# Token mix in three contraction passes over all batches, with mixing matrices transposed in 32x32 blocks on the Vector engine

## The chip, the cores and the metric

The kernel runs on one core of one Trainium2 chip. The metric is the device time of one execution in microseconds (us). Engines are named as the profile names them: PE is the Tensor engine's matmuls, PEld its weight loads (they overlap PE), DVE the Vector engine, ACT the Scalar engine, POOL GpSimd, SP the Sync engine. A name with q at its end (POOLq, SPq) is the sequencer of that engine.

Two words are used throughout. A *block* is 128 rows of the output tokens; there are 33. A *piece* is one block times 384 columns, which is one accumulator tile.

## The reference

Eight batches of 4224 tokens with 192 channels go through a causal depthwise convolution and then through a "phase" mixer.

```python
# x: (8, 4224, 192); weight: (8 heads, 7 taps), softmax over the taps
x = causal_conv(x, softmax(weight))          # 8 groups of 24 channels, one filter each
theta = x @ w_theta                          # 192 x 192
zr, zi = x * cos(theta), x * sin(theta)
y = einsum('ts,bsd->btd', w_tok_r, zr) \
  + einsum('ts,bsd->btd', w_tok_i, zi)       # two 4224 x 4224 matrices
u = x + y
out = u + maximum(u @ w_ch, 0)
```

The token mix is nearly all of the work. It contracts 4224 tokens, twice, for 8 x 192 = 1536 columns. The matrices lie in DRAM as (t, s) in float32. A PE matmul contracts over partitions, so it needs them as (s, t): somebody has to transpose them.

## The kernel before

The kernel before works on four batches at a time, in two rounds. Each round first builds `za_r` and `za_i` for all 4224 tokens of its four batches, and keeps them in SBUF. Then it runs over the 33 blocks. In the first round it transposes the matrices on PE and stores the transposed copy in DRAM. In the second round it loads that copy.

```python
# first round only: transpose 33 tiles of each matrix for the next block
for m, (stage, wt, evac_on_act) in enumerate(((stg_r, wt_r, False), (stg_i, wt_i, True))):
    for base in range(0, NSC, NTG):                      # NTG = 8
        pT = psT2.tile([P, NTG * P], BF16, name="pT", tag="pT")
        for k in range(nb):
            nc.tensor.transpose(pT[:, k * P : (k + 1) * P],
                                stage[:, cch * P : (cch + 1) * P], ident)      # L298
        if evac_on_act: nc.scalar.activation(out=dst, in_=src, func=AT.Copy)   # L306
        else:           nc.vector.tensor_copy(out=dst, in_=src)                # L308
    eng.dma_start(out=wtcache[m, tcc], in_=wt[:])
# ... (both rounds) the mix of one block: 132 matmuls of 384 columns
for cch in range(NSC):                                   # 33
    for m, (wt, zz) in enumerate(((wt_r, za_r), (wt_i, za_i))):
        nc.tensor.matmul(y0, lhsT=wt[:, cch, :], rhs=zz[:, cch, 0:2, :], ...)  # L344
        nc.tensor.matmul(y1, lhsT=wt[:, cch, :], rhs=zz[:, cch, 2:4, :], ...)  # L351
# ... the tail of one block: y + x, 8 PE transposes, matmuls with w_ch, relu, store
```

The line numbers in the comments are those of the profile. Whole file:

## Time and profile before

| Before | |
|---|---|
| time, median of 2 runs | 2003.06 us (2000.9 to 2005.22) |
| span of the profiled run | 1999.5 us |
| PE busy | 1843.1 us, 92% |
| set-up, convolution and phase of batches 0–3 | about 0 to 222 us |
| mix of batches 0–3, with matrix transposes | about 222 to 1119 us |
| phase of batches 4–7 | about 1119 to 1242 us |
| mix of batches 4–7 | about 1242 us to the end |

The stages can be read off the page. Its first part gives the busy time of each engine. Its second part cuts the span into 40 slices of 50 us, and each digit is the busy share in tenths. PEclk is the clock granted to PE in tenths of full speed.

```profile
PE 1843.1 (92%) x13522; PEld 1210.1 (61%) x13522; DVE 488.1 (24%) x1029; ACT 373.2 (19%) x630; POOL 71.6 (4%) x119
...
PE   2666799999999999999999677999999999999998
...
PEclk9888899999999999999999755999999999999999
```

PE is saturated, except in the first five slices and in the three around 1150 us, where the clock falls to half as well. These are the two phase stages. The view by windows puts numbers to a piece of each stage. Its columns are the busy time of each engine (with instruction counts), the clock, the share of the DMA engines' time that is busy, and GB/s.

```profile
core 0: us, PE busy (x) PEld busy (x) DVE busy (x) ACT busy (x) POOL busy (x), PEclk, DMA share, GB/s
700.00:950.00 250.00, 249.03 (x1956) 161.65 (x1955) 48.02 (x90) 43.06 (x54) 9.56 (x18) 1.00 0.71 184
1160.00:1250.00 90.00, 68.43 (x459) 55.41 (x457) 73.68 (x183) 50.59 (x104) 0.00 (x0) 0.54 0.19 54
1400.00:1700.00 300.00, 300.00 (x1961) 184.23 (x1960) 37.74 (x67) 11.80 (x14) 0.00 (x0) 1.00 0.34 126
```

In both mix stages PE leaves next to nothing idle, at full clock. So a shorter mix stage has to come from fewer or shorter PE instructions. The first round has some to give. These are the costliest groups of the matrix transposes (busy us and mean ns, then the idle time of that engine before them and what ended it):

```profile
L306 ACT ACTIVATE wt_i<-pT 128x1024 bf16<-128x1024 bf16 (+1 forms) x165 | 130.1, 884 | 140.2 <-PE pT L298 140.2
...
L298 PE MATMUL pT<-ident,stg_r 128*128 128x128 bf16 x1089 | 90.3, 224 | 8.9 <-DMA stg_r<-in_moe_w_tok_r_dram 8.4
L308 DVE COPY wt_r<-pT 128x1024 bf16<-128x1024 bf16 (+1 forms) x165 | 94.2, 588 | 16.1 <-PE pT L298 16.1
...
L298 PE MATMUL pT<-ident,stg_i 128*128 128x128 bf16 x1089 | 87.0, 218 | 1.4 <-ACT wt_i L306 0.7
```

How long a block takes is best read as the distance between its eviction and that of the next block. The timeline of DVE shows it. Its columns are start, duration, engine, line, operation; the square brackets hold the idle time before. The first two lines are from the first round, the last two from the second:

```profile
1042.61 0.56 DVE L364 TENSOR_TENSOR u_10258<-y_10124,xrt 128x384 f32<-128x384 f32 x1 [21.50 <-PE y_10124 L344]
...
1069.84 0.56 DVE L364 TENSOR_TENSOR u_10518<-y_10384,xrt 128x384 f32<-128x384 f32 x1 [21.50 <-PE y_10384 L344]
...
1512.75 0.56 DVE L364 TENSOR_TENSOR u_14321<-y_14183,xrt 128x384 f32<-128x384 f32 x1 [15.10 <-PE y_14183 L344]
...
1535.45 0.56 DVE L364 TENSOR_TENSOR u_14491<-y_14353,xrt 128x384 f32<-128x384 f32 x1 [15.10 <-PE y_14353 L344]
```

That is 27.2 us per block against 22.7 us, so the transposes cost 4.5 us per block.

**A ledger of PE's time.** For each matmul in the trace, take the time from its start to the start of the next. The Trainium skill ("TensorE: Matmul & The Clock Gate", Back-to-back issue gap) gives N/2.4 + 2.5 ns for N moving columns at full clock, 162.5 ns for N = 384. It means matmuls without the weight loads of a real stream, but the trace agrees: the 132 mix matmuls of a block take 21.5 us, 163 ns each. The sum of N/2.4 + 2.5 over all PE instructions is called the *arithmetic* below. What is spent beyond it is called the *loss*. Loss is then waiting, or matmuls at a lower clock. In the kernel before, the arithmetic is 1726.3 us (1415.8 mix, 121.6 matrix transposes, the rest convolution, phase and tail). The first matmul starts at 14.3 us. The losses of the four stages are 126.9, 34.3, 83.9 and 7.1 us. Where a stage is cut moves some 3 us between it and its neighbour.

### The profile page before, as it was taken

The numbers are of one execution on the slowest core, as the hardware profiler recorded it, in microseconds if no ns is written. First come the engines' busy times: TensorE is split into PE (matmuls) and PEld (weight loads), VectorE is DVE, ScalarE is ACT, GpSimd is POOL, SyncE is SP. The second block draws the span as 40 slices with busy tenths as digits, with TensorE's granted clock in tenths as the row PEclk, the third lists the DMA queues.
The fourth block names the chain that finished last, engine by engine and source line by source line (L and its number), as shares of the span: only waits on it lengthen the run. The fifth ranks groups of instructions, "written<-read, shape, count | busy, mean of one in ns | idle before, by whom it ended". The sixth has DMA issues, their size and how long they took to land.

```text
span 1999.5 us, 30320 instructions
## 1 busy us (share of the span) xinstructions
PE 1843.1 (92%) x13522; PEld 1210.1 (61%) x13522; DVE 488.1 (24%) x1029; ACT 373.2 (19%) x630; POOL 71.6 (4%) x119
## 2 busy tenths in 40 slices
PE   2666799999999999999999677999999999999998
PEld 1655566666666666666666466666666666666665
DVE  7555222221122221122221397111111111111111
ACT  2677311111111111111111165000000000000000
POOL 2111000000000000000000000000000000000000
PEclk9888899999999999999999755999999999999999
DMA  6999766667766667766664321223333323333331
GB/s 103 154 155 153 187 174 174 172 181 192 197 177 171 170 182 192 196 178 169 172 181 147 131 63 48 111 111 111 142 134 112 111 111 143 134 111 111 113 144 37
DMA packets 122179, 287.66 MB, mean 144 GB/s; under 512 B 41776, under 2 KB 96704, under 8 KB 96704
## 3 DMA queue, kind: packets, MB, share of 16 engines
q0 software_dynamic: 44432, 84.58, 25.5%
q1 hardware_dynamic: 63360, 123.29, 17.6%
q10 hardware_dynamic: 14256, 77.86, 9.6%
q8 instruction: 105, 1.72, 0.3%
q14 instruction: 26, 0.21, 0.0%
HBM read 259.94 MB, written 110.30 MB: 185 GB/s over the span
## 4 chain that ended last, share of the span: by engine, by line
PE 82%; issue 9%; DVE 4%; DMA 2%; POOL 2%; ACT 2%; DVEq 0%; POOLq 0%; SPq 0%; ACTq 0%
PE pT L298 5%; PE v L385 2%; POOL xcur L186 1%; PE v L392 1%; PE th_ps L239 1%; DVE xTa L233 1%; PE tU L376 1%; PE th_ps L246 1%; PE tU L377 1%; DMA stg_r<-in_moe_w_tok_r_dram 1%; PE y_12313 L344 1%; PE y_12314 L351 1%; DVE th_sb L254 1%; PE y_10806 L344 1%; PE y_16564 L351 1%
## 5 line engine op out<-in xcount | busy, mean ns | idle before, releaser
L351 PEld LDWEIGHTS <-wt_i 128*128 128x128 bf16 x2178 | 213.2, 98 | 137.3 <-issue 7.1
L344 PEld LDWEIGHTS <-wt_i 128*128 128x128 bf16 x2178 | 213.3, 98 | 130.5 <-issue 0.5
L351 PEld LDWEIGHTS <-wt_r 128*128 128x128 bf16 x2178 | 213.3, 98 | 129.4 <-issue 1.4
L344 PEld LDWEIGHTS <-wt_r 128*128 128x128 bf16 x2178 | 213.3, 98 | 128.6 <-issue 0.3
L306 ACT ACTIVATE wt_i<-pT 128x1024 bf16<-128x1024 bf16 (+1 forms) x165 | 130.1, 884 | 140.2 <-PE pT L298 140.2
L239 PE MATMUL th_ps<-wth_hi,xTa 128*128 128x192 bf16 x264 | 70.4, 313 | 32.5 <-DVE xTa L233 31.9
L298 PE MATMUL pT<-ident,stg_r 128*128 128x128 bf16 x1089 | 90.3, 224 | 8.9 <-DMA stg_r<-in_moe_w_tok_r_dram 8.4
L308 DVE COPY wt_r<-pT 128x1024 bf16<-128x1024 bf16 (+1 forms) x165 | 94.2, 588 | 16.1 <-PE pT L298 16.1
L264 ACT ACTIVATE cs<-th_sb,halfpi 128x384 bf16<-128x384 bf16 x132 | 80.1, 607 | 84.4 <-DVE th_sb L254 84.3
L298 PEld LDWEIGHTS <-stg_i 128*128 128x128 bf16 x1089 | 72.8, 97 | 28.8 <-issue 16.0
L298 PE MATMUL pT<-ident,stg_i 128*128 128x128 bf16 x1089 | 87.0, 218 | 1.4 <-ACT wt_i L306 0.7
L197 PEld LDWEIGHTS <-bands 128*128 128x128 bf16 x264 | 31.1, 118 | 92.0 <-DMA xcur<-in_x_dram 66.7
L298 PEld LDWEIGHTS <-stg_r 128*128 128x128 bf16 x1089 | 71.9, 101 | 17.7 <-DMA stg_r<-in_moe_w_tok_r_dram 8.8
L254 DVE TENSOR_SCALAR th_sb<-th_ps 128x384 bf16<-128x384 f32 x132 | 72.3, 555 | 24.1 <-PE th_ps L246 17.9
L379 DVE COPY uTa<-tU 128x1024 bf16<-128x1024 bf16 x66 | 45.7, 692 | 129.8 <-PE tU L377 129.8
L246 PE MATMUL th_ps<-wth_lo,xTa 128*128 128x192 bf16 x264 | 71.2, 316 | 0.0
L267 ACT ACTIVATE sn<-th_sb 128x384 bf16<-128x384 bf16 x132 | 66.9, 507 | 0.0
L239 PEld LDWEIGHTS <-xTa 128*128 128x128 bf16 x264 | 32.2, 122 | 46.8 <-DVE xTa L233 41.1
L233 DVE COPY xTa<-tTa 128x1024 bf16<-128x1024 bf16 x66 | 45.3, 688 | 55.9 <-PE tTa L231 52.7
L385 PE MATMUL v<-wch_hi,uTa 128*128 128x192 bf16 x264 | 55.6, 250 | 1.6 <-DVE uTa L379 0.8
L392 PE MATMUL v<-wch_lo,uTa 128*128 128x192 bf16 x264 | 55.0, 248 | 0.0
L146 POOL DMA_DIRECT2D stg_r<-in_moe_w_tok_r_dram x33 | 17.6, 533 | 694.1 <-PE pT L298 694.1
(1422 smaller groups left out, 3850.0 us busy)
## 6 DMA issues: line engine op xcount, KB each, us to landing
stg_r<-in_moe_w_tok_r_dram POOLq DMA_DIRECT2D x33, 1056.0 KB, 9.8
stg_i<-in_moe_w_tok_i_dram POOLq DMA_DIRECT2D x33, 1056.0 KB, 16.1
wt_cache<-wt_r SPq DMA_DIRECT2D x33, 1056.0 KB, 19.3
wt_cache<-wt_i ACTq DMA_DIRECT2D x33, 1056.0 KB, 15.4
wt_i<-wt_cache ACTq DMA_DIRECT2D x33, 1056.0 KB, 7.6
wt_r<-wt_cache SPq DMA_DIRECT2D x33, 1056.0 KB, 5.0
out_dram<-osb SPq DMA_DIRECT2D x66, 384.0 KB, 3.1
xcur<-in_x_dram POOLq DMA_DIRECT2D x33, 384.0 KB, 6.7
```

Of the source, the lines that this page charges most:

```text
L239: nc.tensor.matmul(th_ps[:, bb, :], lhsT=xTa[:, 2 * bsrc, :], rhs=wth_hi[:, :], start=True, stop=False,)
L246: nc.tensor.matmul(th_ps[:, bb, :], lhsT=xTa[:, 2 * bsrc + 1, :], rhs=wth_lo[:, :], start=False, stop=True,)
L254: nc.vector.tensor_scalar(out=th_sb, in0=th_ps, scalar1=-CLAMP, scalar2=CLAMP, op0=ALU.max, op1=ALU.min,)
L264: nc.scalar.activation(out=cs, in_=th_sb, func=AT.Sin, bias=halfpi[:], scale=1.0)
L267: nc.scalar.activation(out=sn, in_=th_sb, func=AT.Sin)
L298: nc.tensor.transpose(pT[:, k * P : (k + 1) * P], stage[:, cch * P : (cch + 1) * P], ident,)
L306: nc.scalar.activation(out=dst, in_=src, func=AT.Copy)
L308: nc.vector.tensor_copy(out=dst, in_=src)
L344: nc.tensor.matmul(y0[:, :, :], lhsT=wt[:, cch, :], rhs=zz[:, cch, 0:2, :], start=first, stop=last,)
L351: nc.tensor.matmul(y1[:, :, :], lhsT=wt[:, cch, :], rhs=zz[:, cch, 2:4, :], start=first, stop=last,)
L385: nc.tensor.matmul(v[:, bb, :], lhsT=uTa[:, b_loc, 0:P], rhs=wch_hi[:, :], start=True, stop=False,)
L392: nc.tensor.matmul(v[:, bb, :], lhsT=uTa[:, b_loc, P : 2 * P], rhs=wch_lo[:, :], start=False, stop=True,)
```

## The change

The intent is to take the transposes off PE, and to make the second phase stage disappear. It has four parts.

1. The contraction over 4224 tokens is cut into three passes of 9, 12 and 12 chunks of 128 tokens, with all 1536 columns. The partial sums of a pass go to DRAM in float32 and come back in the next.
2. Only the chunks of one pass need be in SBUF. Those of the next pass are built during the current one, inside the mix.
3. The matrices are transposed on DVE, which turns 32x32 blocks each in place. So that blocks land on the right partitions, a chunk is made of four runs of 32 tokens, one from each quarter of the sequence, and each matrix comes in four loads.
4. The convolution works on windows of 96 tokens with a halo of 16, one matmul per head. Its output makes a round trip through DRAM to reach the order of the chunks.

The diff, cut to its core (cuts are marked `...`):

```diff
-    for p in range(NP):                 # two rounds of four batches
...
-                        nc.tensor.transpose(
-                            pT[:, k * P : (k + 1) * P],
-                            stage[:, cch * P : (cch + 1) * P],
-                            ident,
-                        )
...
-                    eng.dma_start(out=wtcache[m, tcc], in_=wt[:])
...
+    PASSES = (9, 12, 12)
...
+    def conv_round(r):
+        for a in range(NQ):             # NQ = 4 quarters of the sequence
+            t0 = a * SEG + r * WT
+            xw = wk.tile([KW, B, D], BF16, name="xw", tag="xw", bufs=3)
...
+            nc.gpsimd.dma_start(out=xw[lo:KW, :, :], in_=x[...])               # L139
+            xc = wk.tile([WT, B, D], BF16, name="xc", tag="xc")                # 2 buffers
+            for hp in range(H // 2):
...
+                    nc.tensor.matmul(pc[:, hh, :, :], lhsT=bands[:, h, :], ...)   # L148
+                nc.scalar.activation(out=xc[...], in_=pc, func=AT.Copy)        # L152
+            nc.sync.dma_start(out=xs[t0 : t0 + WT, :], in_=xc)
+
+    def phase_chunk(c, wth):
+        xz = wk.tile([P, N], BF16, name="xz", tag="xz")
+        for a in range(NQ):
+            nc.sync.dma_start(out=xz[a * Q : (a + 1) * Q, :], in_=xs[t0 : t0 + Q, :])
...
+            for k in range(3):
+                nc.tensor.transpose(tp[:, k, :], xz[...], ident)               # L174
...
+    def mix_weights(tb, c0, ncs):
+        for m in range(2):
+            for a in range(NQ):
+                nc.gpsimd.dma_start(out=st[a * Q : (a + 1) * Q, ...], in_=w_rows[m][...])  # L214
+            nc.vector.transpose(wt[...], st[...])                              # L221
...
+    def mix(y, wts, zs, c, j, ncs):
+            nc.tensor.matmul(y, lhsT=wts[m][:, c, :, :], rhs=zs[c][m][:, cols], ...)   # L231
...
+    def finish_piece(tb, j, y, p):      # first pass: copy; second: add the partial sum
...
+        nc.gpsimd.tensor_tensor(out=pv, in0=pv, in1=xr, op=ALU.add)            # L254, last pass
+        nc.vector.tensor_tensor(out=ev, in0=y, in1=pv, op=ALU.add)             # L255
+        nc.scalar.activation(out=ub, in_=ev, func=AT.Copy)                     # L257
+        for k in range(3):
+            nc.tensor.transpose(tp[:, k, :], ub[...], ident)                   # L260
+        nc.vector.tensor_copy(out=uT[:], in_=tp[:])                            # L262
+        channel_mix(v, uT, wch)                                                # L198
...
+    def build_round(r):                 # 96 tokens of each quarter = 3 chunks
+        conv_round(r)
+        for c in range(r * CPR, (r + 1) * CPR):
+            zs.append(phase_chunk(c, wth))
...
+            while done < ahead and done * NT <= tb * ahead:
+                build_round(built)      # inside passes 1 and 2, for the next pass
```

## The prediction

> **What bounds the kernel now.** TensorE. The page gives PE 92% busy, DVE 24%, ACT 19%. The timeline splits the 1999.5 us into: band set-up, convolution and phase of half the batches, about 0–225 us; first mix pass, to about 1120 us; phase of the second half, to about 1240 us; second mix pass, to the end. In the mix passes the evictions of successive row blocks lie 27.23 us apart in pass 1 and 22.71 us in pass 2, with PE solid (window table: 249 of 250 us, clock 1.00). The 132 token-mix matmuls of a block take 21.5 us, 163 ns each. The Trainium skill ("TensorE: Matmul & The Clock Gate", Back-to-back issue gap) gives N/2.4 + 2.5 = 162.5 ns for N=384; the trace agrees.
>
> **Removed.** The 2178 PE transposes of the mixing matrices: 27.23 − 22.71 = 4.5 us per block, 33 blocks, about 150 us, all on PE and on the critical path. Their evictions (ACT 130 us, DVE 94 us) and the matrix cache in DRAM (71 MB written, 71 read) were hidden. The second phase stage (PE 68 of 90 us busy at clock 0.54) stops being a stage: it and most of the first are now built inside mix passes. Band set-up (48 DVE ops of 485 ns, last band at 40 us) shrinks to 13 wide ops, perhaps 10 us.
>
> **Unchanged.** 8712 mix matmuls of N=384: 1419 us. No FLOP there is saved.
>
> **Added.**
> - DVE: 198 block transposes of 1152 or 1536 elements per partition. The skill ("VectorE: DVE Perf Modes", The three transpose paths) has 311 ns for 128x128 bf16; no run here shows one. Estimate: one element per cycle, 1.3 and 1.7 us each, about 310 us in all. Piece evictions add 264 x 0.56 us. DVE total about 850 us, half the span: off the critical path.
> - DMA: weights arrive in 101,000 short software descriptors (1152/1536 B read). In the trace x's packets (768 B read) cost about 58 ns of an engine and the 16.9 KB weight rows about 0.72 us; between them, 74–90 ns. Weights about 540 us of 16 engines, x 140; partial sums, out and scratch about 520 (hardware packets fit 17 ns plus bytes at 27 GB/s). Sum 1200 us, about 70% of the span: not the bound on average, but dense enough to delay builds.
> - POOL: 792 weight issues at 0.53 us and 132 adds of perhaps 1 us: about 600 us, hidden.
>
> **The sum.** PE: 1419 mix, 66 phase, 66 finish (3 transposes and 4 matmuls a piece, 0.5 us), 29 convolution = 1580. Start: nine chunks before steady mixing, paced by ACT (1.1 us of sine a piece plus convolution evictions, 1.8 us per piece), end near 100 us, leaving PE idle about 62 us. Tail 8 us. Stalls from late DMA, the last build of pass 2 waiting for z slots, and low clock after gaps: 40 us. Total 1690 us, ratio 0.845. Range 1630–1800, skewed upwards.
>
> **What would show it.** Row blocks about 12.8, 16.7 and 17.7 us apart in the three passes; PE at least 93% busy, clock 1.00 after 100 us; no idle on PE ended by the DVE transposes or weight loads in the steady state; transposes 1.3/1.7 us; DMA share 65–80%.
>
> **What would make it wrong.** Short software descriptors costing twice the estimate (weight DMA then sets the pace, most in pass 1, where partial sums are read and written too); DVE transposes at half rate and evictions queued behind them; in-order PE standing at a build whose DRAM round trip comes later than planned, with the clock falling. These give 1750–1950 us. Slower than before would need DMA near 100% throughout.

## The result, and the profile after

| | before | after |
|---|---|---|
| median, 2 runs each | 2003.06 us (2000.9 to 2005.22) | 1798.86 us (1796.92 to 1800.79) |
| ratio | | 0.898, 95% interval 0.8948 to 0.9013 |

The change is faster by a tenth, 204 us. A ratio here is the mean time of one kernel's fast runs over that of the other's of the same rounds, so it is not quite the ratio of the medians quoted. The prediction said 1690 us, and 1798.86 is at the very edge of its range of 1630 to 1800. There is a gap of 109 us to explain.

The page after, with the two busiest queues of its third part (packets, MB, share of 16 engines):

```profile
PE 1659.7 (92%) x10912; PEld 1016.1 (56%) x10912; DVE 826.6 (46%) x1407; ACT 277.4 (15%) x575; POOL 590.4 (33%) x992
...
PE   2558999989999899999999989999999999999998
...
PEclk9679999999999999999999999999999999999999
...
q0 software_dynamic: 154944, 86.81, 38.7%
q1 hardware_dynamic: 142352, 168.78, 30.1%
```

The hole in the middle is gone, as intended, and so are 2610 PE instructions. PE is still the busy engine. But its row of nines now has eights in it, and the start is still there: a slice of 45 us reads 2, and two more read 5. The windows, in the columns given above:

```profile
50.00:100.00 50.00, 29.26 (x187) 19.95 (x186) 24.32 (x70) 24.11 (x52) 3.29 (x4) 0.69 0.45 86
700.00:800.00 100.00, 95.36 (x623) 58.78 (x622) 47.38 (x82) 18.72 (x40) 26.99 (x49) 0.97 0.74 159
1400.00:1600.00 200.00, 195.74 (x1329) 116.52 (x1328) 97.74 (x151) 22.50 (x43) 86.33 (x131) 1.00 0.70 149
```

Before, the mix stages had PE busy for 249 of 250 and for all of 300 us. After, it is idle for some per cent everywhere. The evictions of each pass give its pace. The line counts 132 of them, with durations in ns and the start of the first and the last:

```profile
L242 DVE COPY ev<-y x132: 517/557/559, 138.1 to 585.7; 128x384 f32<-128x384 f32 x132
...
L249 DVE TENSOR_TENSOR ev<-y,pv x132: 517/557/558, 617.6 to 1174.4; 128x384 f32<-128x384 f32 x132
...
L255 DVE TENSOR_TENSOR ev<-y,pv x132: 517/557/559, 1190.8 to 1792.6; 128x384 f32<-128x384 f32 x132
```

The mean distance between blocks is 13.9, 17.1 and 18.7 us in the three passes. The prediction had 12.8, 16.7 and 17.7. The first piece is finished at 138.1 us; the prediction had the start over near 100. The ledger puts the four stages side by side:

| us | start idle before the first matmul | arithmetic | loss, start | loss, passes | after the last matmul | sum |
|---|---|---|---|---|---|---|
| after | 16.3 | 1576.0 | 85.2 | 36.3 + 41.5 + 39.0 = 116.7 | 4 | 1799 |
| prediction | (in the start) | 1580 | 62 | 40 | 8 | 1690 |

(Parts are rounded one by one; the start ends at the first eviction, and 0.7 us of loss in the very last tail is in no column.) Where PE waits in the start and in the first two passes is in the view of waits: engine and line, what it waited for, us in total, times, longest.

```profile
PE tp L174 <- DMA xz<-xs: 40.9, 10, 10.3
PE pc L148 <- DMA xw<-in_x_dram: 24.7, 10, 3.1
PE pc L148 <- ACT xc L152: 17.4, 25, 2.5
PE pc L148 <- DVE bands L126: 16.3, 1, 16.3
```

The last is the set-up of the filter bands, once at the start. The other three belong to the building of chunks: the round trip through DRAM, the convolution's x tiles, and its evictions. The trace shows one such round, in the middle of the second pass:

```profile
895.63 0.32 PE L231 MATMUL y<-zi,wt_8638 128*128 128x384 bf16 x1
898.18 0.37 PE L148 MATMUL pc<-xw,bands 112*96 112x192 bf16 x2 [2.23 <-DMA xw<-in_x_dram]
...
900.57 0.48 PE L148 MATMUL pc<-xw,bands 112*96 112x192 bf16 x2 [1.36 <-ACT xc L152]
...
901.48 0.52 PE L231 MATMUL y<-zr,wt_8631 128*128 128x384 bf16 x1
901.80 0.52 PE L231 MATMUL y<-zi,wt_8638 128*128 128x384 bf16 x1
```

PE stands 2.23 us at a convolution matmul whose x tile has not landed, then 1.36 us for a convolution buffer, though it has plenty of mix matmuls whose inputs are there. (In the source a whole convolution round stands before the mix of a block; in the trace convolution and mix matmuls alternate. So the order on PE is laid out when the program is built.) The Trainium skill ("TensorE: Matmul & The Clock Gate", Step-by-step: what each phase is for) says that matmuls stay in program order and that only weight loads are pulled ahead. This is what it looks like. The second half of the cost follows at once: mix matmuls start 320 ns apart instead of 162.5, since the clock is halved. In the window from 901 to 906 us the clock reads 0.50. The same page (What's actually happening) gives the reason: the gate halves the clock after an idle window of about 3.4 us and restores it after about as long a busy stretch. The trace agrees on the length: in passes 1 and 2 its stretches at half clock last 3.41 or 6.83 us, about 48 us in all. It doesn't agree that the whole window has to be idle. The clock fell at 899.3 us, after the first wait and before the second was over, and in the 3.41 us before that PE had stood for 2.6 us (from the starts in the trace, each matmul counted as N/2.4 + 2.5 ns). Before all 15 falls of this run it had stood for 2.0 to 3.1 us. Windows on the same grid of 3.41 us that the clock outlasted had at most 2.1 us. So here about 2 us of waiting, in one piece or in several, was enough.

The last pass builds nothing, so its loss must be something else. There the loss is small each time and very regular:

```profile
1400.51 1.78 DVE L221 STREAM_TRANSPOSE wt_14039<-st_14034 128x1536 bf16<-128x1536 bf16 x1 [1.23 <-PE y L231]
1402.83 0.52 ACT L257 ACTIVATE ub<-ev 128x384 bf16<-128x384 f32 x1 [5.52 <-DVE ev L255]
1402.91 0.33 PE L231 MATMUL y<-zi,wt_13840 128*128 128x384 bf16 x1
1403.40 0.34 PE L260 MATMUL tu<-ident,ub 128*128 128x128 bf16 x3 [0.17 <-ACT ub L257]
1403.58 0.33 PE L231 MATMUL y<-zr,wt_13833 128*128 128x384 bf16 x1
```

The tail's transposes start 0.49 us after the mix matmul in front of them, not 0.16. They need `ub`, which ACT finishes at 1403.35. In the ledger, the step from a mix matmul to these transposes loses 34.1 us, in 131 cases. In 95 of them it is 224 to 231 ns. The case shown is one of 30, one piece in most blocks, with 0.33 us: there the eviction `ev` stood right behind the transpose of a mixing matrix on DVE, the first line. That tenth of a microsecond, some 3 us in all, is what the new DVE work costs the tail. It doesn't make the rest: e10 below has no such transposes on DVE, and the same step loses 37.0 us there in 128 cases. The view of waits shows only 6.8 us of it, since modelled ends of matmuls overlap what comes next. Here the starts have to be read.

### The profile page after: what moved, and what is told of

Read it like the earlier page. It is cut to its first block, busy times and chain, and to the rows that moved or that the text cites. A ratio compares the mean times of both kernels' runs of the same rounds, so it can differ in the third digit from the quotient of the medians.

```text
span 1799.1 us, 28540 instructions
## 1 busy us (share of the span) xinstructions
PE 1659.7 (92%) x10912; PEld 1016.1 (56%) x10912; DVE 826.6 (46%) x1407; ACT 277.4 (15%) x575; POOL 590.4 (33%) x992
## 2 busy tenths in 40 slices
DMA packets 297433, 257.41 MB, mean 143 GB/s; under 512 B 69200, under 2 KB 288848, under 8 KB 297296
## 3 DMA queue, kind: packets, MB, share of 16 engines
q0 software_dynamic: 154944, 86.81, 38.7%
q1 hardware_dynamic: 142352, 168.78, 30.1%
## 4 chain that ended last, share of the span: by engine, by line
PE 71%; DMA 9%; DVE 8%; ACT 6%; issue 5%; DVEq 0%; SPq 0%; ACTq 0%; POOL 0%; POOLq 0%
PE y L231 62%; DMA xs<-xc 6%; DVE ev L255 4%; ACT ub L257 4%; PE th L198 3%; PE tu L260 2%; DMA xz<-xs 2%; PE v L198 2%; ACT xc L152 1%; PE pc L148 1%; PE tp L174 1%; DVE ang L182 1%; DVE zr L190 1%; DVE xT L178 1%; DVE zi L191 0%
## 5 line engine op out<-in xcount | busy, mean ns | idle before, releaser
L254 POOL TENSOR_TENSOR pv<-pv,xr 128x384 f32<-128x384 f32 x132 | 120.6, 914 | 336.7 <-issue 161.9
L152 ACT ACTIVATE xc<-pc 96x384 bf16<-96x384 f32 x176 | 77.0, 482 | 661.1 <-PE pc L148 606.1
L249 DVE TENSOR_TENSOR ev<-y,pv 128x384 f32<-128x384 f32 x132 | 72.1, 548 | 223.3 <-PE y L231 202.1
L257 ACT ACTIVATE ub<-ev 128x384 bf16<-128x384 f32 x132 | 69.0, 523 | 539.4 <-DVE ev L255 539.4
L242 DVE COPY ev<-y 128x384 f32<-128x384 f32 x132 | 71.8, 547 | 153.6 <-PE y L231 153.4
L255 DVE TENSOR_TENSOR ev<-y,pv 128x384 f32<-128x384 f32 x132 | 72.2, 548 | 129.1 <-PE y L231 129.1
L266 DVE SCALAR_TENSOR_TENSOR ov<-v,ev 128x384 f32<-128x384 f32 x132 | 73.3, 555 | 65.0 <-PE v L198 60.3
L188 ACT ACTIVATE sn<-ang 128x384 bf16<-128x384 f32 x132 | 67.9, 515 | 202.5 <-DVE ang L182 202.4
L189 ACT ACTIVATE cs<-ang,half_pi 128x384 bf16<-128x384 f32 x132 | 79.1, 599 | 110.4 <-DVE zr L190 110.4
L174 PE MATMUL tp<-ident,xz 128*128 128x128 bf16 x396 | 40.3, 239 | 40.9 <-DMA xz<-xs 40.9
L198 PE MATMUL th<-wth,xT 128*128 128x192 bf16 x528 | 67.8, 265 | 9.0 <-DVE xT L178 7.2
L182 DVE TENSOR_SCALAR ang<-th 128x384 f32<-128x384 f32 x132 | 70.6, 550 | 12.0 <-PE th L198 10.6
```

Source lines behind the costliest of these rows:

```text
L152: nc.scalar.activation(out=xc[:, :, hp * 2 * G : (hp + 1) * 2 * G].rearrange("p b (h g) -> p h b g", h=2, g=G), in_=pc[:, :, :, :], func=A ...
L174: nc.tensor.transpose(tp[:, k, :], xz[:, j * PC + k * P : j * PC + (k + 1) * P], ident)
L182: nc.vector.tensor_scalar(out=ang, in0=th[:, :, :].rearrange("p b d -> p (b d)"), scalar1=-CLAMP, scalar2=CLAMP, op0=ALU.max, op1=ALU.min,)
L189: nc.scalar.activation(out=cs, in_=ang, func=AT.Sin, bias=half_pi[:], scale=1.0)
L198: nc.tensor.matmul(dst[:, b, :], lhsT=tT[:, b + k, :], rhs=w[:, 2 * b + k, :], start=(k == 0), stop=(k == 1),)
L254: nc.gpsimd.tensor_tensor(out=pv, in0=pv, in1=xr, op=ALU.add)
```

## The experiments

Ten kernels were run, in three groups; each was timed in rounds with the kernel before. The kernel before measured 2001.64 to 2003.37 us in these groups, so medians can be compared across them to 0.1%. Losses are from the ledger, read for every kernel in the same way.

The theories at the start. **A: PE's order.** PE runs in order, and instructions that depend on something late stand in its way: the tail's transposes, the convolution, the phase chunks. **B: DMA supply.** More than twice the DMA packets of before (297,433 against 122,179) and a DMA share of about 69% make everything late, and what waits is a symptom. **C: the estimate of the transposes was wrong**, and taking them off PE is worth less than 150 us.

### e1: the tail of a piece, one piece later

```diff
+        late.append((rows, cols, j, ev, ub))     # after ub; transposes, w_ch and store moved out
...
                     finish_piece(tb, j, y, p)
+                    finish_late(1)               # runs the tail of the piece before
```

> The new kernel, but in the last pass the three transposes and the channel mix of a piece come after the next piece's mix in program order. Theory A (TensorE takes its instructions in order and stands at those whose inputs come later than the order assumed): of 39 us that TensorE loses in the last pass, 34 us lie in front of the 131 tail transposes, which wait for ScalarE's copy; they go, and the time falls by 25 to 34 us from 1799, to 1765-1774. Theory B (the DMA supply of short software descriptors is what makes things late): this touches no DMA, so the time stays within 5 us.

Measured: 1797.29 us (1795.81 to 1798.18), ratio 0.897 [0.8956, 0.8984]. This was a miss: 1.6 us instead of 25 to 34. The trace says why:

```profile
1400.95 0.33 PE L269 MATMUL tu<-ident,ub 128*128 128x128 bf16 x3
...
1401.79 0.35 DVE L271 COPY uT<-tu 128x384 bf16<-128x384 bf16 x1
...
1402.19 0.28 PEld L198 LDWEIGHTS <-uT 128*128 128x128 bf16 x4 [0.49 <-DVE uT L271]
1402.20 0.50 PE L198 MATMUL v<-wch,uT 128*128 128x192 bf16 x4
```

The transposes now start on time. But the channel mix behind them needs their eviction `uT`, and that is now what is late. In the ledger, 34.1 us in front of 131 transposes became 33.5 us in front of 132 channel mixes. The wait only moved one link along the chain. That is a failed experiment with a lesson: the tail has two such links, and both have to be stretched. It also left a rival alive: that PE loses about 0.25 us each time for a change of instruction shape, wherever it stands. e6 tests that.

### e2: one more x tile and one more convolution output

```diff
-    masks = bpool.tile([KW, KS, WT], BF16, name="masks")
+    masks = wk.tile([KW, KS, WT], BF16, name="masks", tag="xz")      # to make room
...
-            xw = wk.tile([KW, B, D], BF16, name="xw", tag="xw", bufs=3)
+            xw = wk.tile([KW, B, D], BF16, name="xw", tag="xw", bufs=4)
...
-            xc = wk.tile([WT, B, D], BF16, name="xc", tag="xc")
+            xc = wk.tile([WT, B, D], BF16, name="xc", tag="xc", bufs=3)
```

> The new kernel with four instead of three buffers for the x tiles and three instead of two for the convolved tiles (two set-up tiles share slots to make room). Theory A: in each of the eight convolution rounds inside the passes TensorE stands 2-4 us for the fourth x tile, which finds no buffer until the round has begun, and 1.4-2.5 us for an eviction that waits for a buffer; then the clock is halved for 3.4-6.8 us. These go: 30 to 55 us less, 1745-1770. Theory B: buffers add no bandwidth; under 10 us less.

Measured: 1788.31 us (1784.39 to 1791.87), ratio 0.8925 [0.8905, 0.8946]. That is 11 us less than the kernel after: short of theory A's 30 to 55 and about what theory B allowed, so the time alone decides nothing. The waits of PE do:

```profile
PE tp L174 <- DMA xz<-xs: 77.6, 11, 12.7
...
PE pc L148 <- ACT xc L152: 4.0, 19, 0.3
```

The convolution hardly waits any more: for x not at all, for its buffers 4.0 us instead of 17.4. In the ledger the step from mix to convolution lost 17.6 and 19.4 us in passes 1 and 2 and now loses 2.7 and 2.6. But the wait for the chunks that come back from DRAM grew from 40.9 to 77.6 us. The four convolutions were finished sooner, and PE then stood at the first chunk for as long as the round trip took: the step from mix to a chunk's transposes lost 24.9 and 19.0 us in passes 1 and 2, where it had lost 10.4 and 5.4.

### e3: the convolution one round ahead

```diff
     def build_round(r):
-        conv_round(r)
+        if r + 1 < NR:
+            conv_round(r + 1)
         for c in range(r * CPR, (r + 1) * CPR):
             zs.append(phase_chunk(c, wth))
...
-    for c in range(CPR):
-        zs.append(phase_chunk(c, wth))
-    for r in range(1, built):
+    for r in range(built):
         build_round(r)
```

> The new kernel with every convolution round put one round ahead of the phase stage that reads it back from DRAM. Theory A: the waits of the phase transposes for the tokens' round trip through DRAM go: 27 us of the start and 16 us of the first two passes, with some half-clock time after them; 25 to 50 us less, 1750-1775, and the first eviction comes before 115 us instead of 138. The x waits of the convolution stay. Theory B: no change beyond 10 us.

Measured: 1759.24 us (1753.18 to 1760.68), ratio 0.8783 [0.8767, 0.8799]; as expected. The wait for `xz` fell from 40.9 to 3.6 us, and the half-clock time in passes 1 and 2 from about 48 to about 24 us. The first eviction came at 127.8 us, 10 us earlier; under 115 was expected, so the start moved less. (The edit also moves one of the eight convolution rounds out of the passes into the start.) What is left is the other kind of wait, as e2 would have it:

```profile
PE pc L148 <- DMA xw<-in_x_dram: 28.2, 12, 3.2
...
PE tp L174 <- DMA xz<-xs: 3.6, 2, 2.3
```

### e5: both

This is e2 and e3 in one kernel.

> The convolution one round ahead and the extra buffers of the second run together, on the new kernel. After the second run TensorE stood longer for the tokens' round trip instead (25 and 19 us in the first two passes, 10 and 5 without the buffers), after the third it stood for the x tiles (15 and 9 us). Theory A: the two waits stand one behind the other, and taken away together their savings are more than the sum of 10 and 40 us: 1720-1740. Theory B (DMA supply): no more than the third run, 1750-1765.

Measured: 1725.01 us (1724.38 to 1728.88), ratio 0.8618 [0.8606, 0.8631]; as expected. Against the kernel after, e2 brought 11 us, e3 40, and both together 74. The two waits stand one behind the other in PE's order, so removing one hands much of its time to the next. Passes 1 and 2 now lose 17.2 and 8.8 us instead of 36.3 and 41.5.

### e6: the tail in three steps

```diff
+        late.append((rows, cols, j, ev, ub))
+
+    def finish_late(keep):
+        while later:
+            finish_channels(*later.pop(0))        # w_ch and store of the piece before the last
+        while len(late) > keep:
+            later.append(turn(*late.pop(0)))      # transposes and uT of the last piece
...
                     finish_piece(tb, j, y, p)
+                    finish_late(1)
```

> The last pass's tail in three steps: transposes of a piece after the next piece's mix, channel mix after the mix of the one behind it. The first run only moved the wait from the transposes (34 us) to the channel mix (33.5 us of 132 waits of 0.25 us). Theory A': the order is laid out so that each instruction comes at the moment its input is planned to be ready, and the chip is 0.25 us late on this chain; with a whole piece of slack on both steps neither is waited for: 25 to 34 us less, 1764-1774. Rival: it is a cost of the change of shape on TensorE, not a wait; then it stays, 1790 or more.

Measured: 1763.85 us (1760.01 to 1766.37), ratio 0.8805 [0.8788, 0.8823]; as expected, 35 us less than the kernel after. The loss of the last pass fell from 39.0 to 1.5 us; that of passes 1 and 2 stayed (36.6 and 41.5). The channel mix and the transposes are still there and still change shape, but nothing waits:

```profile
1403.28 0.33 PE L231 MATMUL y<-zi,wt 128*128 128x384 bf16 x1
1403.45 0.49 PE L198 MATMUL v<-wch,uT 128*128 128x192 bf16 x4
...
1403.78 0.33 PE L271 MATMUL tu<-ident,ub 128*128 128x128 bf16 x3
1403.94 0.33 PE L231 MATMUL y<-zr,wt 128*128 128x384 bf16 x1
```

From one start to the next it is 0.17 us, 0.33 us for four channel matmuls, 0.16 us for three transposes. The rival, a cost of changing shape, is refuted. The waits were for the inputs.

### e8: the matrices loaded only once

```diff
+            new = m not in kept
+            if new:
+                kept[m] = constp.tile([P, NQ, NCMAX * Q], BF16, name=f"st{m}")
+            st = kept[m]
-            for a in range(NQ):
+            for a in range(NQ if new else 0):
                 nc.gpsimd.dma_start(...)
```

All blocks use the same weights, so the result is wrong. All DVE transposes stay.

> The new kernel with the mixing matrices loaded once and kept, all block transposes still done (wrong result on purpose): about 97,000 of 101,000 short descriptors go, DMA share falls from 68% to about 40%. Theory B (DMA supply makes things late): at least 60 of the 117 us lost in the passes go, 1740 or less. Theory A (order and buffers): x loads no longer queue behind weights, so their waits shorten, but the tail's 34 us and most round trips stay: 10 to 40 us less, 1760-1790.

Measured: 1777.8 us (1776.9 to 1779.26), ratio 0.8879 [0.8865, 0.8892]. The software queue went from 38.7% to 8.2% of the DMA engines' time, and the kernel gained 21 us. The losses of the passes are still 27.4, 30.9 and 37.8 us. So theory B is refuted as the main cause. Crowded DMA explains about a fifth of the gap, most of it in passes 1 and 2, where chunks are built. The regular loss of the last pass does not depend on it.

### e7: all three

This is e5 and e6 in one kernel. The result is correct.

> Convolution ahead, extra buffers and the three-step tail together. If the savings add: 1690-1712, which is the time predicted for the change; TensorE's loss in the three passes falls from 117 us to under 35.

Measured: 1689.62 us (1688.8 to 1694.53), ratio 0.8443 [0.8428, 0.8458]. The gains of e5 (74) and e6 (35) add up to the 109 us measured, as they should if they are about different passes. It is 6% faster than the kernel after and the fastest of all. The page:

```profile
PE 1618.2 (96%) x10912; PEld 1024.7 (61%) x10912; DVE 808.5 (48%) x1407; ACT 278.7 (17%) x575; POOL 590.4 (35%) x992
...
PE   3679999999999999999999999999999999999998
...
PEclk9989999999999999999999999999999999999999
```

### e4: the kernel before, with DVE transposes

This kernel keeps the two rounds, the phase stages and the cache of the kernel before, and changes only who transposes. The blocks come from four quarters but the tokens are not put in that order, so the result is wrong.

```diff
-                for base in range(0, NSC, NTG):
-                    ...
-                        nc.tensor.transpose(pT[...], stage[...], ident)
-                    ...                                   # evictions by ACT and DVE
+                for base in range(0, NSC, 11):
+                    nc.vector.transpose(wt[:, base : base + 11, :]..., stage[...]...)
```

(The loads of `stg_r` and `stg_i` become four each, one for each quarter.)

> The kernel before with one part of the change alone: the PE transposes of the mixing matrices and their evictions replaced by 32x32 block transposes on VectorE, the matrices loaded in four quarters with 4.2 KB rows; wrong result on purpose, since the tokens' order in z isn't changed to match. Theory A: the 66 transposes per block cost 4.5 us of TensorE in 33 blocks, and nothing takes their place: 150 us less than 2003, 1840-1870. Rival: VectorE's transposes (about 9 us a block) or the shorter descriptors hold up the blocks and give a third or more back: 1890 or more.

Measured: 1903.34 us (1901.15 to 1906.3), ratio 0.9501 [0.9484, 0.9518]. Only 99 us less than the kernel before. So in the old frame, theory C's side was met: the transposes were not worth 150 us there. But they did leave PE, and the ledger shows what came in their place. The loss of the first mix pass rose from 34 to 52 us, and from the eleventh block on PE stands once in each block:

```profile
700.68 0.56 DVE L359 TENSOR_TENSOR u<-y,xrt 128x384 f32<-128x384 f32 x1 [11.47 <-issue]
...
701.62 3.16 DVE L296 STREAM_TRANSPOSE wt_i<-stg_i 128x1408 bf16<-128x1408 bf16 x2
702.70 0.23 PE L371 MATMUL tU<-ident,u 128*128 128x128 bf16 x1 [1.62 <-ACT u L366]
703.31 0.34 PE L339 MATMUL y<-za_i,wt_i 128*128 128x384 bf16 x1
```

DVE had stood idle for 11.47 us, and the next block's `wt_i` is transposed only after this block's eviction. The next block has two matmuls with `wt_r`, at 700.59 and 700.75 us, and then needs `wt_i`. PE stands at the old block's tail transposes in the meantime, 1.78 us in each of 22 blocks, 39.2 us in all (the expectation of e9 below counts 21 and 37.5). There is one staging buffer for each matrix, so the load of the next block can't start before the transposes of this one end. But in the block shown the load was not late: the last part of `stg_i` landed at 693.8 us, 7 us before the eviction.

### e9: e4 with two staging buffers

```diff
-            stg_r = stgp.tile([P, 4, S // 4], BF16, name="stg_r", tag="stg_r", bufs=1)
+            stg_r = stgp.tile([P, 4, S // 4], BF16, name="stg_r", tag="stg_r", bufs=2)
```

(The same for `stg_i`; `xrp` goes from 2 buffers to 1 to make room. The result is wrong, as in e4.)

> The kernel before with block transposes on VectorE as in the fourth run, with two staging buffers per matrix instead of one (the x residual gets one instead of two, to make room); wrong result on purpose. In the fourth run each block from the eighth on stood 1.8 us (37.5 us in 21 blocks) at the tail's transposes: the imaginary matrix was block-transposed only after the next block's mix had begun to need it, its staging buffer being free too late. Theory: single staging gave back the missing third; with two buffers TensorE's loss in the first pass falls from 52 to under 20 us and the time from 1903 to 1860-1880. Rival: VectorE's transposes sit in front of the evictions whatever the staging; no change, 1895-1905.

Measured: 1872.54 us (1864.79 to 1873.28), ratio 0.9348 [0.9328, 0.9368]; as expected in time. It is 129 us less than the kernel before of the same group. The loss of the first mix pass went from 52 to 32 us; under 20 was expected, so part of the cause is still in there. The trace shows it: in ten blocks, from 757 us on, PE stands 1.78 to 2.13 us at the tail transposes just as in e4, 18.2 us in all, though `stg_i` has landed before. So the second buffer halved the number of such blocks. It did not remove what puts the transposes of `wt_i` behind the eviction.

### e10: the kernel after, with PE transposes

```diff
-            wt = wpool.tile(...)
-            nc.vector.transpose(wt[...], st[...])
+            for b0 in range(0, ncs, 6):
+                pT = trps.tile([P, 6, P], BF16, name="pT", tag="pT", bufs=1)
+                for k in range(nb):
+                    nc.tensor.transpose(pT[:, k, :], st[:, c * P : (c + 1) * P], ident)
+                ...                                       # evictions by DVE and ACT
```

The loads become one a matrix. The transposed accumulators are split, one bank for these and one for the others. The order of the tokens doesn't fit the chunks, so the result is wrong.

> The new kernel with one part undone: the mixing matrices transposed on TensorE again, 2178 transposes of 128x128, evicted by VectorE and ScalarE (one PSUM bank for them and one instead of two for the other transposes; chunks take 128 consecutive staged columns, so the token order is wrong on purpose). If the transposes are worth what their issue time is: 2178 x 55.8 ns = 121 us more, and with waits at the evictions 120-160 us more: 1920-1960. If VectorE's transposes cost the new kernel something in turn (late evictions), the difference is below 110 us, under 1910.

Measured: 1947.59 us (1942.49 to 1949.2), ratio 0.9726 [0.9708, 0.9745]; as expected. That is 149 us more than the kernel after. In the ledger the arithmetic is 121.6 us larger (1697.6 against 1576.0), and the losses make up the rest, about 25 us. These 25 us are not the transposes' alone: this kernel also has one bank fewer for the other transposes. With that reserve the estimate of 150 us holds in the new frame, and theory C is refuted there: with the transposes still on PE, the change would have been worth less than 3%.

### The ledger of all kernels

| loss in us | start | pass 1 | pass 2 | pass 3 | median time |
|---|---|---|---|---|---|
| after | 85.2 | 36.3 | 41.5 | 39.0 | 1798.86 |
| e1, tail one piece later | 85.1 | 34.6 | 40.5 | 36.5 | 1797.29 |
| e2, more buffers | 81.8 | 40.1 | 32.6 | 38.3 | 1788.31 |
| e8, matrices loaded once | 82.6 | 27.4 | 30.9 | 37.8 | 1777.8 |
| e6, tail in three steps | 84.7 | 36.6 | 41.5 | 1.5 | 1763.85 |
| e3, convolution ahead | 71.7 | 22.1 | 22.3 | 38.2 | 1759.24 |
| e5 = e2 and e3 | 62.1 | 17.2 | 8.8 | 38.3 | 1725.01 |
| e7 = e5 and e6 | 63.5 | 15.0 | 8.4 | 1.7 | 1689.62 |
| e10, transposes on PE | 94.9 | 39.7 | 42.8 | 49.1 | 1947.59 |

The arithmetic is 1576 us in all of them but e10. So each row can be checked: 16.3 + 1576 + its losses + about 4 gives the span of the profiled run to within 2 us, and the time of that run is 1.7 us more than its span.

## Why the prediction was right or wrong

**Right: what bounds it, and why the change pays.** PE bounds both kernels, at 92% busy. The prediction's PE total of 1580 us measured 1576.0. In the ledger, the 200 us between the two profiled runs are 150 us less arithmetic (121.6 of it the transposes) and 50 us less loss (252.2 before, 201.9 after). The transposes are worth "about 150 us" in the new frame, as e10 shows (149, with the reserve made there). In the old frame they are worth less, 99 us with one staging buffer and 129 with two (e4, e9), because the DVE order put a wait back, in 22 blocks and in ten. That the phase stage of the second half stops being a stage is in the page: the hole near 1150 us, with a loss of 83.9 us, is gone.

**Right: what would be hidden.** DVE is busy for 827 us (850 predicted), POOL for 590 (600). A transpose of 1152 elements per partition has a median of 1.370 us and one of 1536 of 1.769 us (1.3 and 1.7). The software queue's 38.7% of 1799 us is 696 us of 16 engines (540 + 140 predicted), and the hardware queue's 30.1% is 541 (520). The sum is 69% of the span (70%). In steady state PE never stood for a mixing matrix, as predicted. "Evictions queued behind them" did happen, in 30 pieces of the last pass, at 0.1 us each. The two other reasons given for a very slow result, short descriptors at twice the estimate and transposes at half rate, did not happen.

**Wrong: "Stalls from late DMA, the last build of pass 2 waiting for z slots, and low clock after gaps: 40 us."** These measured 116.7 us. This is the largest mis-sized term, 77 of the 109 us. Three causes were in it. The first the prediction did not have; the other two it named and set too low. The wait for z slots hardly shows: the last three chunks get theirs at 1168 to 1185 us, and around them PE loses about 4 us in four waits.

- The tail of the last pass lost about 37 us. The prediction counted only its PE instructions, 0.5 us a piece, and no wait. Its chain is eviction on DVE, copy on ACT, transposes on PE, eviction on DVE, channel mix on PE. The laid-out order puts the PE instructions where their inputs come about 0.23 us too late (0.33 in 30 of 131 cases). e1 moved the wait, e6 removed it.
- The convolution rounds inside passes 1 and 2 stood for x tiles and output buffers, then for a round trip through DRAM. In e5, with one more buffer for each and the convolution a round ahead, the loss of these two passes falls from 77.8 to 26.0 us.
- The clock after these waits, about 48 us at half speed. As half speed doubles the time of a matmul (320 ns for 162.5), that is an estimate of at most 24 us of loss, contained in the losses above; the 158 matmuls that lie wholly in these stretches make 20 of it. The prediction named it, and its size in e3 falls by half with the waits.

"In-order PE standing at a build whose DRAM round trip comes later than planned, with the clock falling" stands in the prediction, but as a reason for a bad case. It was the normal case.

**Wrong: "Start: ... end near 100 us, leaving PE idle about 62 us."** The first eviction came at 138.1 us. The idle time was 16.3 us before the first matmul plus 85.2 us of loss, 101.5 us, 39.5 us more. The prediction took ACT as the pacemaker of the start, at 1.8 us a piece. In the first slices ACT is no busier than DVE or PE (24.1 of the 50 us from 50 to 100 us). The start was paced in part by the same waits for x and for the round trip: e5 brought the first eviction to 118.4 us and the loss to 62.1, which is 23 of the 39.5 us. What paces the rest was not tested. The wait for the band set-up was 16.3 us where "perhaps 10" was predicted, and no run changed it.

**The sum.** The four terms miss by −4 (arithmetic), +39.5 (start), +76.7 (stalls) and about −4 (end), which makes the 109 us. That the median still fell inside the range is the width of the range and luck: it lies 1.1 us from the edge, and one of the two runs, with 1800.79 us, lies outside. e7 ends at 1689.62 us, the time predicted. That is a coincidence in part: its passes lose less than the 40 us predicted (25.1) and its start more than 62 (16.3 + 63.5 = 79.8).

**The signs.** Blocks 12.8, 16.7 and 17.7 us apart: missed by the kernel after (13.9, 17.1, 18.7), met within 0.3 us by e7 (12.7, 16.4, 17.6). PE at least 93%: missed by a point. Clock 1.00 after 100 us: wrong, it falls in every round of building.

**What stays open.** Why the laid-out order is 0.23 us early at the tail: that the order was planned with durations shorter than the chip's is only inferred, and no run looked at the plan. Whether the 63.5 us left at the start can be hidden. What the 14 us of loss in e9's first pass are that its ten waits leave, and why in e4 and e9 the second matrix's transpose was placed behind the eviction though DVE was idle before.

## What to carry to other kernels

When PE is the bound and is to stay busy, count for each PE instruction not only its time but when its inputs are there; every instruction that depends on another engine or on DMA should stand at least one whole piece of independent matmuls behind the thing it needs, and a chain with two such links needs two such distances. Buffers and order go together: a buffer alone (11 us) or an earlier issue alone (40 us) moved the wait to the next link, and both brought 74 us. To predict, don't enter stalls as a round sum: list the rounds in which work is built inside a saturated stage, and give each the wait that its load or round trip takes in the trace, and more for the halved clock where PE waits 2 us or longer within 3.4 us. In passes 1 and 2 here that was about a third on top: 20 us on 58.

## What the Trainium skill lacked or had wrong

- "VectorE: DVE Perf Modes", The three transpose paths: the section has one size, 311 ns for 128x128 bf16. Wide instructions measured 1.370 us for 1152 and 1.769 us for 1536 elements per partition, which makes 1.04 ns an element and about 0.17 us beside (worked out from the two). From this 128 elements would take 303 ns, so the one size fits. A rate per element stands elsewhere in the skill. The page calls 32x32 blocks useful for some layouts and useless for others; here four loads, one for each quarter of the sequence, made them serve as full transposes.
- "TensorE: Matmul & The Clock Gate", Part 4: PE-mode transpose: the page has 275 to 390 ns for a 128x128 transpose and says that the full clock doesn't engage for it. In the kernel before, the mean of one is 218 to 224 ns, and 16 of them pass in 0.89 us between mix matmuls. That is about 56 ns each, the full-clock gap for 128 columns. So in a stream of matmuls they do run at full clock; whether transposes alone would bring it about, no run shows.
- Same page, Back-to-back issue gap: the page says that in a real stream of weight loads and matmuls the formula counts too much at large N (131 ns for N = 512). Here each mix matmul has its own weight load, and N = 384 takes 163 ns, the formula's value, over whole passes.
- Same page, What's actually happening: it speaks of an idle window of about 3.4 us and has no figure for a window that is idle in part. In the run of the kernel after, the clock fell after windows of 3.41 us with 2.0 to 3.1 us idle, and stayed after windows with up to 2.1.
- "DMA: Bandwidth & Descriptors": it has no cost of a short packet of the software queue that casts float32 to bfloat16. Here 154,944 packets took 38.7% of 16 engines' span of 1799.1 us, 71.9 ns of an engine each. By size, those of the weights took 75.9 ns (576 B written) and 90.3 ns (768 B) on average, those of x 54.7 ns (384 B), in a queue that shares the engines with another.
- "Perfetto Trace Analysis", Optimization Strategy: it says that consistent bubbles on the engine that should be saturated can mean too little SBUF or PSUM for the next tile. e2 and e5 agree for the convolution's x tiles. But the most regular bubble, 0.23 or 0.33 us before nearly all of 131 pieces, was no lack of buffers: it was the order of instructions on PE, and e6 removed it. The section doesn't name this cause, and it was not found on another page.
